# The attention's second products in three float32r passes for items 4 to 15

## The chip, the cores and the metric

One core of one Trainium2 chip runs the whole program. The time is the device time in microseconds of one execution; the time before is the median of three runs.

## The reference, cut to what matters

The kernel computes a linear attention, a mixture of eight experts with Sinkhorn-normalised gates, and a SwiGLU block, one behind the other, all in float32. The change touches the attention alone:

```python
def _attn_ref(q, k, v):            # 4 batches, 8 heads, 576 rows, 64 wide
    q_s = exp(q - max(q, axis=-1)); q_s = q_s / (sum(q_s, axis=-1) + 1e-9)
    k_s = exp(k - max(k, axis=2));  k_s = k_s / (sum(k_s, axis=2) + 1e-9)
    kv = einsum('bhsd,bhse->bhde', k_s, v)
    return einsum('bhsd,bhde->bhse', q_s, kv)
```

The last line is the product in question: each row of the softmaxed q times the 64x64 matrix kv of its head.

## The kernel before

The attention is cut into 16 items, each one batch and two heads. For an item, kv of the two heads is kept as one 128x128 block-diagonal tile (kvbd), and q is transposed to q^T, 128 partitions (two heads of 64) by two halves of 288 rows. The second product is then two float32 matmuls with kvbd as the weights and 288 moving columns each (x_mm, line 628), into two PSUM tiles px.

An item passes through small steps, each a function of its own: k_partial_max (m, line 471), q_max (qm, L480), q_sub (L489), k_max (a transpose on TensorE, L500), k_max2 (kmx, L507), k_spread (a matmul that needs kmx, L516), k_sub (ke, L523), the two exponentials (L511 and L532), k_sum, kv_mm (L566), k_total (L578), k_recip (kr, L586 and L587), kv_scale (kb, L596), q_norm (qs, L538 to L542), q_mul, q_T (transposes into two PSUM tiles pq, L606), q_T2 (c, L618), x_mm (X, L628), x_hi and x_lo (copies out of px, L643 to L650).

The order of the work on every engine is the order in which the program emits it (a manual schedule), and each engine's instructions run in that order. Items 0 to 3 are prepared by a list written out by hand (START). For items 4 to 15 a row of four strings (STEPS) is repeated, in which the number behind a step's name says how many items back it works:

```python
STEPS = (
    "D-1 ke-1 eq-1 ek-1 s-1", "G-2 K-2 kr-2 kb-2 m-0 T-2 qm-0 qp-0", "c-2 qs-1 qn-1",
    "B-0 kx-0 X-2 xh-2 xl-2",
)
```

These strings are laid between the units of the first expert layer: a unit h (two tiles ph_a of 12 float32r matmuls, relu on ScalarE into hh, L842, and on VectorE into hl, L843) and a unit y (four tiles py of 6 matmuls each; VectorE or ScalarE adds py into slot_e or a late tile, L905 and L903). One string goes ahead of each unit, one into the middle of a unit h, three behind the first three tiles of a unit y. Between them also stand the splits of weights into a high and a low part (split: a ScalarE copy to float32r, L94, and a VectorE subtract, L95; wsh_a, wsl_a, w2h, w2l) and the gates (L664 and L674, eight narrow matmuls each, copied out by L667 and L677).

The expert matmuls use mm3 (lines 97 to 100): for operands in two float32r parts it makes three passes, high by high, high by low, low by high. PSUM has two py tiles, two ph tiles, one pk and one pv tile, and two tiles of the pool psq, which pq and px share. Outside the START list px n takes the buffer in which pq n stood. qT has one buffer, kvbd two (even and odd items).

Of the kernel before, what the change touches and what calls it, by code (L numbers as in the profile page):

```python
# [8 lines left out]
F32 = mybir.dt.float32  # L9
F32R = mybir.dt.float32r  # L10
U32 = mybir.dt.uint32
AF = mybir.ActivationFunctionType
ALU = mybir.AluOpType
# [5 lines left out]
def kernel(  # L19
# [23 lines left out]
    nc = tc.nc  # L43
    nc = tc.nc
    B, H, S, D = q.shape
# [3 lines left out]
    P = 128  # L49
    SP = 96  # L50
    SC = S // SP
    H2 = S // 2
# [40 lines left out]
    def split(hi, lo, src, eng=None):  # L93
        nc.scalar.copy(hi, src)  # L94
        (eng or nc.vector).tensor_tensor(lo, src, hi.bitcast(F32), op=ALU.subtract)  # L95

    def mm3(ps, lh, ll, rh, rl, first, last):
        nc.tensor.matmul(ps, lh, rh, start=first, stop=False, skip_group_check=True)  # L98
        nc.tensor.matmul(ps, lh, rl, start=False, stop=False, skip_group_check=True)  # L99
        nc.tensor.matmul(ps, ll, rh, start=False, stop=last, skip_group_check=True)  # L100
# [13 lines left out]
    def bank(kind, cols, name):  # L114
        turn = BANK[kind]
        turn.append(turn.pop(0))
        pool = turn[-1]
        if isinstance(pool, str):
            return pb_tile(pool, name)[:, :cols]
        return pool.tile([P, cols], F32, tag="p", name=name)  # L120
# [317 lines left out]
    ap_ = attn.enter_context(tc.tile_pool(name="attn", bufs=2))  # L438
# [5 lines left out]
    }  # L444

    kvbd = []
    for i in range(2):
        t = ap_.tile([P, P], F32, tag=f"kvbd{i}", name=f"kvbd{i}", bufs=1)
        nc.gpsimd.memset(t, 0.0)
        kvbd.append(t)  # L450

    ITEMS = [(b, g) for b in range(B) for g in range(H // HG)]
# [137 lines left out]
    def kv_scale(i):  # L590
        st = ST[i]
        pkv, kr = st["pv"][:, :P], st["kr"]
        kv = kvbd[i % 2]
        for h in range(2):
            r = slice(h * D, (h + 1) * D)
            nc.scalar.activation(kv[r, r], pkv[r, r], AF.Copy, scale=kr[r])  # L596
        st["kv"] = kv

    def q_T(i):

# [12 lines left out]

    def q_T2(i):
        st = ST[i]
        qT = ap_.tile([P, 2, H2], F32, tag="qT", name=f"qT_{i}", bufs=1)
        for n, pq in enumerate(st["pq"]):
            nc.scalar.copy(qT[:, n], pq[:, :H2])  # L618
        st["qT"] = qT

    def x_mm(i, early=False):

        st = ST[i]
        st["px"] = []
        for n in range(2):
            nm = f"px_{i}_{n}"
            px = bank("y", 512, nm) if early else psq.tile([P, 512], F32, tag="pq", name=nm)
            nc.tensor.matmul(px[:, :H2], st["kv"], st["qT"][:, n], start=True, stop=True)  # L628
            st["px"].append(px)

    def x_parts(i, g0):
# [432 lines left out]
    def unit2_y(u, hook):  # L1064
# [22 lines left out]
    OPS = dict(  # L1087
        m=k_partial_max, B=k_max, kx=k_max2, D=k_spread, ke=k_sub, ek=k_exp, s=k_sum,
        G=kv_mm, K=k_total, kr=k_recip, kb=kv_scale, qm=q_max, qp=q_sub, eq=q_exp,
        qs=q_norm, qn=q_mul, T=q_T, c=q_T2, X=x_mm, xh=x_hi, xl=x_lo,  # L1090
    )

# [63 lines left out]
    for n, key in enumerate(keys):  # L1156
# [4 lines left out]
        i = 6 if kd == "a" else 13  # L1161
        if u >= NU and group(u)[0] == 0:
            i = 2 if kd == "a" else 5
# [105 lines left out]
    with tc.manual_schedule():  # L1269
# [59 lines left out]
        for step in START.split():  # L1329
            op, i = step.split("-")  # L1330
            if op in WOPS:
                WOPS[op](int(i))
            elif op == "X":
                x_mm(int(i), True)
            else:
                OPS[op](int(i))
# [23 lines left out]
        for i in range(13):  # L1360
            for j, st in enumerate(STEPS):
                if i == 0 and j == 0:
                    st = st.replace("D-1 ", "")
# [12 lines left out]
        n = 0  # L1376
# [82 lines left out]
```

## Time and profile before

| what | value |
|---|---|
| median of three runs | 2041.18 us (2040.77 to 2044.21) |
| the profiled execution | 2042.81 us |
| its span, first to last instruction | 2040.2 us |
| mean granted TensorE clock | 0.997 |
| TensorE matmul (PE) | 2011.4 us busy, 99% |
| TensorE weight load (PEld) | 1742.1 us, 85% |
| VectorE (DVE) | 1414.0 us, 69% |
| ScalarE (ACT) | 777.8 us, 38% |
| GpSimd (POOL) | 412.9 us, 20% |
| the chain that ended last | PE 94%, DVE 4%, ACT 1%, issue 1% |

Times in the trace are microseconds from the span's start. A matmul's record is longer than its turn on the engine: matmuls are pipelined, and the ends are modelled, so the distance between starts tells what one costs. An arrow in square brackets says how long an engine stood still before an instruction and what ended the wait.

### The profile page before, as it was taken

The page shows a single profiled execution, that of the slowest core. Times are in us where ns is not written, and L with a number is a line of the kernel's source. Part 1 is how long each engine was busy: PE and PEld are TensorE (multiplying, and loading weights), DVE is VectorE, ACT ScalarE, POOL GpSimd, SP SyncE. Part 2 cuts the span into 40 slices and gives each one's busy share as a digit, 9 for nine tenths or more (in the row PEclk, how much of TensorE's full clock was granted, in tenths as well). Part 3 has the DMA queues.
Part 4 walks back from the last instruction along what each step waited for, and adds up shares of the span by engine and source line. Part 5 has one row for each costly group of instructions (what it writes and reads, how often), then busy time and mean ns, then how long its engine had stood idle before and what let it go on. Part 6 is the DMA issues. An engine that isn't in the chain of part 4 may idle for free.

```text
span 2040.2 us, 25609 instructions
## 1 busy us (share of the span) xinstructions
PE 2011.4 (99%) x9522; PEld 1742.1 (85%) x9522; DVE 1414.0 (69%) x2178; ACT 777.8 (38%) x1374; POOL 412.9 (20%) x388
## 2 busy tenths in 40 slices
PE   7999999999999999999999999999999999999999
PEld 6888878888888888888888888888888888888887
DVE  8785787766767777776658878878764546565455
ACT  5454323335434334333343333333332243432432
POOL 5451000022222222222113223223220000110110
PEclk9999999999999999999999999999999999999999
DMA  8443222345666555565677778778874747656542
GB/s 206 128 126 104 83 93 93 99 147 196 224 241 220 197 205 205 210 222 206 224 286 263 263 261 289 275 273 292 283 263 156 273 153 259 226 201 260 199 159 77
DMA packets 154237, 415.09 MB, mean 203 GB/s; under 512 B 13569, under 2 KB 66305, under 8 KB 153729
## 3 DMA queue, kind: packets, MB, share of 16 engines
q1 hardware_dynamic: 154112, 413.47, 58.3%
q8 instruction: 74, 1.21, 0.2%
q14 instruction: 51, 0.41, 0.1%
HBM read 281.69 MB, written 131.73 MB: 203 GB/s over the span
## 4 chain that ended last, share of the span: by engine, by line
PE 94%; DVE 4%; ACT 1%; issue 1%; DMA 0%; POOL 0%; DVEq 0%; POOLq 0%; ACTq 0%
PE py L98 13%; PE py L99 12%; PE py L100 12%; PE b_a L100 10%; PE b_a L98 10%; PE b_a L99 10%; PE ph_a L98 3%; PE ph_a L100 3%; PE ph_a L99 3%; PE po L100 2%; PE po L99 2%; PE po L98 2%; PE b_v L98 2%; PE b_v L100 2%; PE b_v L99 2%; PE pv L566 1%
## 5 line engine op out<-in xcount | busy, mean ns | idle before, releaser
L98 PE MATMUL py<-w2h,hh 128*128 128x512 f32 x1152 | 453.7, 394 | 3.4 <-DVE slot_e L905 1.9
L99 PE MATMUL py<-w2l,hh 128*128 128x512 f32 x1152 | 450.0, 391 | 0.0
L100 PE MATMUL py<-w2h,hl 128*128 128x512 f32 x1152 | 449.5, 390 | 0.0
L781 ACT COPY u_a<-b_a 128x448 f32<-128x448 f32 x228 | 121.6, 533 | 693.9 <-PE b_a L100 693.8
L98 PEld LDWEIGHTS py<-w2h,hh 128*128 128x128 f32 x1152 | 216.7, 188 | 47.6 <-DVE slot_e L905 2.1
L100 PEld LDWEIGHTS py<-w2h,hl 128*128 128x128 f32 x1152 | 216.8, 188 | 45.9
L99 PEld LDWEIGHTS py<-w2l,hh 128*128 128x128 f32 x1152 | 216.9, 188 | 42.8
L98 PE MATMUL b_a<-sT,wsh_a 128*128 128x448 f32 x608 | 220.1, 362 | 3.3 <-DVE c L795 2.1
L100 PE MATMUL b_a<-sT,wsl_a 128*128 128x448 f32 x608 | 220.7, 363 | 0.0
L99 PE MATMUL b_a<-sT,wsh_a 128*128 128x448 f32 x608 | 220.3, 362 | 0.0
L909 DVE SCALAR_TENSOR_TENSOR slot_a<-py,Pm,slot_a 128x512 f32<-128x512 f32 x217 | 162.5, 749 | 52.2 <-PE py L100 50.2
L909 DVE SCALAR_TENSOR_TENSOR slot_b<-py,Pm,slot_b 128x512 f32<-128x512 f32 x217 | 161.2, 745 | 23.5 <-PE py L100 22.5
L100 PE MATMUL b_a<-sB,wsl_a 128*128 128x448 f32 x456 | 165.7, 363 | 0.2 <-DMA wsl_a<-wdl_a 0.2
L99 PE MATMUL b_a<-sB,wsh_a 128*128 128x448 f32 x456 | 165.2, 362 | 0.0
L98 PE MATMUL b_a<-sB,wsh_a 128*128 128x448 f32 x456 | 165.2, 362 | 0.0
L95 DVE TENSOR_TENSOR w2l<-w2r,w2h 128x512 fp32r<-128x512 f32 x162 | 117.9, 728 | 41.3 <-ACT w2h L94 41.3
L843 DVE SCALAR_TENSOR_TENSOR hl<-c,hh 128x896 fp32r<-128x896 f32 x128 | 143.2, 1119 | 0.9 <-ACT hh L842 0.7
L805 POOL TENSOR_TENSOR c<-u_a,p_a 128x448 f32<-128x448 f32 x64 | 73.9, 1155 | 344.4 <-ACT u_a L781 344.3
L240 POOL TENSOR_TENSOR sum<-w1r 128x256 f32<-128x256 f32 x32 | 23.8, 744 | 570.8 <-DMA w1r<-in_moe_w_dram 261.8
L842 ACT ACTIVATE hh<-c 128x896 fp32r<-128x896 f32 x128 | 122.4, 956 | 28.0 <-POOL c L805 28.0
L94 ACT CAST w2h<-w2r 128x512 fp32r<-128x512 f32 x162 | 97.1, 618 | 92.1 <-PE py L100 83.2
L98 PEld LDWEIGHTS b_a<-sT,wsh_a 128*128 128x128 f32 x608 | 113.8, 187 | 13.2 <-DVE c L795 3.7
(232 smaller groups left out, 3680.5 us busy)
## 6 DMA issues: line engine op xcount, KB each, us to landing
w2r<-in_moe_w_dram SPq DMA_DIRECT2D x96, 512.0 KB, 4.5
w1r<-in_moe_w_dram SPq DMA_DIRECT2D x64, 512.0 KB, 3.4
wsdh<-wsh_a SPq DMA_DIRECT2D x32, 896.0 KB, 6.5
wsdl<-wsl_a SPq DMA_DIRECT2D x32, 896.0 KB, 7.9
wsh_a<-wsdh SPq DMA_DIRECT2D x32, 896.0 KB, 6.5
wsl_a<-wsdl SPq DMA_DIRECT2D x32, 896.0 KB, 8.5
w2d<-w2l SPq DMA_DIRECT2D x32, 512.0 KB, 2.9
w2l<-w2d SPq DMA_DIRECT2D x32, 512.0 KB, 5.1
```

The lines of the kernel that those rows point to most:

```text
L94: nc.scalar.copy(hi, src)
L95: (eng or nc.vector).tensor_tensor(lo, src, hi.bitcast(F32), op=ALU.subtract)
L98: nc.tensor.matmul(ps, lh, rh, start=first, stop=False, skip_group_check=True)
L99: nc.tensor.matmul(ps, lh, rl, start=False, stop=False, skip_group_check=True)
L100: nc.tensor.matmul(ps, ll, rh, start=False, stop=last, skip_group_check=True)
L240: nc.gpsimd.tensor_tensor(s1, a21, a22, op=ALU.add)
L566: nc.tensor.matmul(st["pv"][:, :P], st["ke"][:, c].rearrange("p h d -> p (h d)"), st["v"][:, :, c, :], start=(c == 0), stop=(c == SC - 1),)
L781: nc.scalar.copy(tmp[n], bk[i])
L805: nc.gpsimd.tensor_tensor(c[:, 1, 1], tmp["u3"], tmp["p5"], op=ALU.add)
L842: nc.scalar.activation(th, src, AF.Relu)
L843: return lambda: nc.vector.scalar_tensor_tensor(tl, src, 0.0, th.bitcast(F32), op0=ALU.max, op1=ALU.subtract)
L909: nc.vector.scalar_tensor_tensor(a, py, pe, a, op0=ALU.mult, op1=ALU.add)
```

## The change

For items 4 to 15 kv and q^T are each kept in two float32r parts, and x_mm makes three passes of mm3 for each half in place of one float32 matmul. kv_scale writes the high part on ScalarE and then, for each half of the diagonal, the low part on VectorE, in one scalar_tensor_tensor that scales again and subtracts. q_T2 calls split for each half. The two new kv tiles, kh and kl, have one buffer each; ql has one. Items 0 to 3 work as before, with q^T in the tile that is now declared float32r and used as float32.

```diff
     kvbd = []
-    for i in range(2):
-        t = ap_.tile([P, P], F32, tag=f"kvbd{i}", name=f"kvbd{i}", bufs=1)
-        nc.gpsimd.memset(t, 0.0)
+    for i in range(4):
+        t = ap_.tile([P, P], F32 if i < 2 else F32R, tag=f"kvbd{i}", name=f"kvbd{i}", bufs=1)
+        nc.gpsimd.memset(t if i < 2 else t.bitcast(F32), 0.0)
         kvbd.append(t)
...
     def kv_scale(i):
...
+        kh, kl = kvbd[2:]
         for h in range(2):
             r = slice(h * D, (h + 1) * D)
-            nc.scalar.activation(kv[r, r], pkv[r, r], AF.Copy, scale=kr[r])
-        st["kv"] = kv
+            nc.scalar.activation(kh[r, r], pkv[r, r], AF.Copy, scale=kr[r])
+            nc.vector.scalar_tensor_tensor(
+                kl[r, r], pkv[r, r], kr[r], kh[r, r].bitcast(F32), op0=ALU.mult, op1=ALU.subtract
+            )
+        st["kv"] = kh, kl
...
     def q_T2(i):
...
+        qT = ap_.tile([P, 2, H2], F32R, tag="qT", name=f"qT_{i}", bufs=1)
+        ql = ap_.tile([P, 2, H2], F32R, tag="ql", name=f"ql_{i}", bufs=1)
         for n, pq in enumerate(st["pq"]):
-            nc.scalar.copy(qT[:, n], pq[:, :H2])
-        st["qT"] = qT
+            split(qT[:, n], ql[:, n], pq[:, :H2])
+        st["qT"] = qT, ql
...
     def x_mm(i, early=False):
...
-            nc.tensor.matmul(px[:, :H2], st["kv"], st["qT"][:, n], start=True, stop=True)
+            if i < 4:
+                nc.tensor.matmul(px[:, :H2], st["kv"], st["qT"][:, n], start=True, stop=True)
+            else:
+                (kh, kl), (qh, ql) = st["kv"], st["qT"]
+                mm3(px[:, :H2], kh, kl, qh[:, n], ql[:, n], True, True)
```

## Rows read from the trace of the kernel before

**Rows 1.** Windows, 49 to 189 us: length, busy of PE, PEld, DVE, ACT, POOL, clock, DMA.

```profile
49.00:189.00 140.00, 136.60 (x761) 115.75 (x759) 103.13 (x178) 70.91 (x156) 60.84 (x54) 0.98 0.37 113
```

**Rows 2.** Waits, 50 to 190 us: total, times, longest.

```profile
PE py L98 <- DVE slot_e L905: 1.9, 2, 1.3
PE py L98 <- DVE late L905: 1.2, 1, 1.2
...
DVE hl L843 <- ACT hh L842: 12.8, 8, 2.6
```

**Rows 3.** Timeline of TensorE: start us, us, engine line op; item 14, and ph_a.

```profile
175.29 1.13 PE L628 MATMUL px<-qT,kvbd 128*128 128x288 f32 x4
176.26 0.28 PE L674 MATMUL pg<-wg,slot_b 128*128 128x8 f32 x2
...
61.29 0.40 PE L98 MATMUL ph_a<-slot_a,wsh_a 128*128 128x512 f32 x1
61.52 0.39 PE L99 MATMUL ph_a<-slot_a,wsh_a 128*128 128x512 f32 x1
```

**Rows 4.** Instructions of lines 650 and 843: duration ns min/median/max, starts, shape.

```profile
L650 DVE TENSOR_TENSOR slot_a<-px,slot_a x8: 359/412/425, 23.8 to 35.1; 128x256 fp32r<-128x256 f32 x8
...
L843 DVE SCALAR_TENSOR_TENSOR hl<-ph_a,hh x64: 676/691/693, 39.1 to 445.9; 128x512 fp32r<-128x512 f32 x64
```

**Rows 5.** Timeline of item 9, 111.5 to 115 us: VectorE, ScalarE, TensorE's px.

```profile
111.55 0.16 DVE L587 RECIPROCAL kr<-kr 128x1 f32<-128x1 f32 x1
111.63 1.53 DVE L471 TENSOR_REDUCE m<-k 96x128 f32<-96x768 f32 x1
...
111.80 0.63 ACT L596 ACTIVATE kvbd<-pv,kr 64x64 f32<-64x64 f32 x2 [2.16 <-DVE kr L587]
...
112.46 0.70 ACT L618 COPY qT<-pq 128x288 f32<-128x288 f32 x2
...
113.08 0.93 DVE L480 TENSOR_REDUCE qm<-q 96x12 f32<-96x768 f32 x1
...
113.56 1.16 PE L628 MATMUL px<-qT,kvbd 128*128 128x288 f32 x4
...
113.94 0.67 DVE L905 TENSOR_TENSOR slot_e<-py,slot_e 128x512 f32<-128x512 f32 x1
...
114.54 0.93 DVE L538 TENSOR_REDUCE qs<-qe 96x12 f32<-96x768 f32 x1
```

**Rows 6.** Timelines of VectorE and TensorE, item 4: kmx and its reader.

```profile
54.32 0.25 DVE L507 TENSOR_REDUCE kmx<-pk 128x1 f32<-128x96 f32 x1
...
54.62 0.46 PE L516 MATMUL pk<-ident,kmx 128*96 128x128 f32 x2
```

**Rows 7.** Timelines of VectorE and TensorE, item 5.

```profile
64.23 0.69 DVE L843 SCALAR_TENSOR_TENSOR hl<-ph_a,hh 128x512 fp32r<-128x512 f32 x1 [1.62 <-ACT hh L842]
...
69.00 0.50 PE L98 MATMUL py<-w2h,hh 128*128 128x512 f32 x1 [0.64 <-DVE slot_e L905]
```

**Rows 8.** Timelines of VectorE and TensorE, item 6.

```profile
75.44 0.67 DVE L905 TENSOR_TENSOR slot_e<-py,slot_e 128x512 f32<-128x512 f32 x1
...
76.71 1.16 PE L628 MATMUL px<-qT,kvbd 128*128 128x288 f32 x4
```

**Rows 9.** Timelines of VectorE and TensorE, items 7 and 13: evictions and py.

```profile
88.55 0.69 PE L98 MATMUL py<-w2h,hh 128*128 128x512 f32 x1 [1.26 <-DVE slot_e L905]
...
163.05 0.68 DVE L905 TENSOR_TENSOR late<-py,late 128x512 f32<-128x512 f32 x1
...
163.78 0.50 PE L98 MATMUL py<-w2h,hh 128*128 128x512 f32 x1
```

**Rows 10.** Windows, a stretch at half clock (columns as in rows 1).

```profile
88.70:92.10 3.40, 3.40 (x9) 2.56 (x10) 2.35 (x7) 0.00 (x0) 2.40 (x2) 0.50 0.37 105
```

**Rows 11.** Timeline of GpSimd at the start.

```profile
1.35 0.20 POOL L449 MEMSET kvbd<- 128x128 f32 x1
...
6.38 1.47 POOL L489 TENSOR_TENSOR qe<-q,qm 96x768 f32<-96x768 f32 x1 [4.83 <-DVE qm L480]
```

More of the change, by code (lines that the diff above doesn't have):

```diff
@@ L592, in kv_scale @@
         pkv, kr = st["pv"][:, :P], st["kr"]
-        kv = kvbd[i % 2]
+        if i < 4:
+            kv = kvbd[i % 2]
+            for h in range(2):
+                r = slice(h * D, (h + 1) * D)
+                nc.scalar.activation(kv[r, r], pkv[r, r], AF.Copy, scale=kr[r])
+            st["kv"] = kv
+            return
+        kh, kl = kvbd[2:]
         for h in range(2):
             r = slice(h * D, (h + 1) * D)
-            nc.scalar.activation(kv[r, r], pkv[r, r], AF.Copy, scale=kr[r])
-        st["kv"] = kv
+            nc.scalar.activation(kh[r, r], pkv[r, r], AF.Copy, scale=kr[r])
[3 more added lines that the diff above has]
+        st["kv"] = kh, kl
     def q_T(i):
@@ L615, in q_T2 @@
         st = ST[i]
-        qT = ap_.tile([P, 2, H2], F32, tag="qT", name=f"qT_{i}", bufs=1)
+        if i < 4:
+            qT = ap_.tile([P, 2, H2], F32R, tag="qT", name=f"qT_{i}", bufs=1).bitcast(F32)
+            for n, pq in enumerate(st["pq"]):
+                nc.scalar.copy(qT[:, n], pq[:, :H2])
+            st["qT"] = qT
+            return
+        qT = ap_.tile([P, 2, H2], F32R, tag="qT", name=f"qT_{i}", bufs=1)
+        ql = ap_.tile([P, 2, H2], F32R, tag="ql", name=f"ql_{i}", bufs=1)
         for n, pq in enumerate(st["pq"]):
-            nc.scalar.copy(qT[:, n], pq[:, :H2])
-        st["qT"] = qT
+            split(qT[:, n], ql[:, n], pq[:, :H2])
+        st["qT"] = qT, ql
     def x_mm(i, early=False):
@@ L627, in x_mm @@
             px = bank("y", 512, nm) if early else psq.tile([P, 512], F32, tag="pq", name=nm)
-            nc.tensor.matmul(px[:, :H2], st["kv"], st["qT"][:, n], start=True, stop=True)
+            if i < 4:
+                nc.tensor.matmul(px[:, :H2], st["kv"], st["qT"][:, n], start=True, stop=True)
+            else:
+                (kh, kl), (qh, ql) = st["kv"], st["qT"]
+                mm3(px[:, :H2], kh, kl, qh[:, n], ql[:, n], True, True)
             st["px"].append(px)
```

## The prediction

> **What bounds the kernel now.** I read the attention stretch first, because the change touches nothing else: 49 to 189 us holds the work of items 4 to 15. TensorE is busy 136.60 of those 140 us and VectorE 103.13 [rows 1]. By busy time TensorE is the bound and VectorE has room; the next views say why that is not the whole story. The list of waits shows three waits of TensorE, all for evictions of py, 3.1 us together, while VectorE's own largest is 12.8 us, for ScalarE's relu in front of hl [rows 2]. So VectorE idles mostly at one kind of place, and a delay on its queue costs nothing only if that place comes before TensorE next needs it. The timelines around single items answer that, item by item.
>
> **The products themselves.** An item's two f32 products stand as four records of 288 columns; they begin at 175.29 and the next matmul's at 176.26, so 0.97 us [rows 3]. The new item has six float32r passes of 288 columns. A float32r pass of 512 columns follows the last after 0.23 us [rows 3]. The columns alone at 2.4 GHz are 0.213 and 0.120 us; with the same 0.013 to 0.017 us on top, 288 columns come to 0.133 us. Bounds: 0.129 (0.23 by the share of columns) and 0.23 (no gain for fewer columns); I take 0.133, as the columns set the 0.23. Six are 0.80 us: 0.17 us less per item, 2.0 us for twelve items, if nothing waits.
> The Trainium skill ("TensorE: Matmul & The Clock Gate", section "Back-to-back issue gap") gives N/2.4 + 2.5 ns when warm, so 122.5 ns for 288 columns and an estimated 0.235 us an item, 2.8 us in all. It gives 216 ns for 512 columns where the row has 230, so I keep the row.
>
> **The added VectorE work.** kv_scale now emits, per half, a ScalarE write of kh and a VectorE scalar_tensor_tensor of kl, 64x64 from PSUM. Nearest rows: a reciprocal of one column 0.16 us, a reduce over 96 columns 0.25 us; I take 0.20. q_T2 adds two subtracts of 128x288 from PSUM. The same operation on 256 columns takes 0.41 us, a scalar_tensor_tensor of 512 takes 0.69 [rows 4]: 0.45 by the line between, bounds 0.41 and 0.69. Back to back a VectorE instruction starts some 0.08 us before its predecessor ends (row 113.08, 0.93 long, against 113.94) [rows 5], so each subtract costs 0.37 us of queue.
>
> **What that does to the queue.** Item 9 [rows 5]. The reciprocal of kr ends at 111.71 and today m starts at 111.63. ScalarE's two kvbd writes run from 111.80 to 112.43. New: kl of the first half can start only after 112.11, that of the second after 112.43, so it ends near 112.43 + 0.04 + 0.20 = 112.67, and m, next in VectorE's order, starts near 112.60. **The step kb costs VectorE 0.97 us**, more than half of it standing still for ScalarE, with everything behind it (m, qm, evictions, hl). **The step c costs 2 x 0.37 = 0.74 us** more, emitted ahead of qs.
> X needs both: today it needs qT, which ScalarE had at 113.16. New, m, qm and the eviction at 113.94 end 0.97 us later, at 115.58, and the two subtracts end at 115.95 and 116.32. The px tiles take the two PSUM banks in which pq stood (two buffers), and the subtract now reads pq, so the three passes of px 0 start after the first subtract and those of px 1 after the second. The last three end at 116.37 + 2 x 0.133 + 0.30 = 116.94, where 0.30 is the 0.39 of a 512-column record less 224 columns at 2.4 GHz. Today px ends at 114.72. TensorE is in order, so all of its work moves by **+2.2 us**.
>
> The other items, each taken from a point where both engines are equally late (VectorE waits for TensorE or ScalarE again before the next kr):
> - Items 4 and 10: kmx ends at 54.57 and the k_spread matmul that needs it starts at 54.62 [rows 6]. kmx is behind both steps, so TensorE stands 0.97 + 0.74 = 1.71 us longer. Two items: +3.4.
> - Items 5, 8, 11, 14: VectorE waits 1.62 us in front of hl [rows 7], which swallows the 0.97 (14 has no m behind it). The subtracts then go in after hl, and the eviction for which TensorE already waits 0.64 us at 69.00 comes 0.74 us later. Four items: +3.0. 8 and 11 have kmx close before the spread instead, for the same price.
> - Item 6: the eviction of 75.44 moves to 76.41, the second subtract ends near 77.82 and px near 78.43 where it ended at 77.87 [rows 8]: +0.6.
> - Item 7: TensorE waits 1.26 us for the eviction at 88.55 [rows 9], which is behind kb but ahead of c: 0.97 - 0.17 = +0.8.
> - Item 13: the eviction that ends at 163.73 is followed by the py matmul at 163.78 [rows 9] and stands behind both steps: +1.7.
> - Items 12 and 15: qT is made long before X, so the faster passes show: -0.3 together.
> Sum: 2.2 + 3.4 + 3.0 + 0.6 + 0.8 + 1.7 - 0.3 = **+11.4 us**.
>
> **The clock.** In this part TensorE ran twice for some 3.4 us at 1.2 GHz; in the first of them it was busy all of the 3.40 us at a granted clock of 0.50 [rows 10], so it cost half of that, 1.7 us. Each time it fell while TensorE was waiting for an eviction, behind narrow gate matmuls; after the shorter wait of item 5 it did not fall. The change adds waits as long as these (item 9's, item 4's), so I count two more: +3.4 us; bounds none and four.
>
> **Costed at nothing.** Two more memsets on GpSimd, 0.20 us each: its next work waits 4.83 us for qm at 6.38 [rows 11]. Without that cover they would cost 0.4 us. The q^T of the first four items changes only its declared type. kh and kl are one pair where there were two kvbd tiles, but kb of an item is emitted after X of the item before, and waits for a later matmul of TensorE anyway. After 189 us no operation changes, and TensorE stays the engine in front, so the loss should stay. No DMA is added or moved; loads issued behind k_sub and kv_mm move with those.
>
> **Sum.** 11.4 + 3.4 = 14.8 us. The profiled execution took 2042.81 us (span 2040.2), 1.63 above the median of the three runs; against the median 2041.18 that is 2056 us.
>
> **Rivals.**
> A, hidden: VectorE has 37 us without work in the stretch, about 3 an item, against 1.7 added. If its idle time falls between each delay and TensorE's next need, only the passes show: 2041.2 - 2.0 = 2039.2. For it: items 5 and 8, where the wait before hl takes up the first delay. Against it: kmx, 0.05 us ahead of its reader, and item 9, where VectorE runs without a gap from kr to qs. It decides at the subtracts of c: if ql is there when X begins, A holds.
> B, half: the delays overlap more than I add (a late TensorE lets VectorE catch up, subtracts at their lower bound) and no clock is lost: half of 11.4, 2047.
> C, faster: A holds, and moving the evictions also removes both half-clock stretches: 2039.2 - 2 x 1.7 = 2035.8. For it: these depend on where waits fall. Against it: both sit behind evictions that now come later.
> D, the passes aren't cheaper: at 0.23 us each, six cost 1.38 against 0.97. Where X waits, three passes after the last subtract cost 0.3 more; elsewhere it is 0.6 an item: about 5 us on top, 2061.
>
> **How the numbers follow.** 0.2% is 4.1 us, about what a measurement of this kernel can tell from no change. Chances: my forecast 0.64, B 0.10, D 0.06 (all slower: 0.80), A 0.15 (within), C 0.05 (faster). The range runs from 2044, between A and B, to 2064: above, the clock's bound adds 3.4 and the subtracts' bound (0.69 for 0.45, felt by some nine items twice) up to 4.3, the lesser pass prices the rest. Left out are A and C, 0.20.
>
> **What would show it.** In the changed profile: px as six records an item, near 0.13 us apart where nothing waits; kl starting some 0.4 us after the reciprocal, and m 0.97 us later against it; TensorE waits named after ql in front of px, about 2 us for item 9; kmx in front of L516 and L905 in front of py with larger totals than the 3.1 us; further stretches at 1.2 GHz. I'd be wrong if px followed its predecessor without a gap in items 4, 9 and 10, or if m kept its place right behind the reciprocal.

## The result and the profile after

The changed kernel is slower: 2063.41 us (median of four runs, 2060.81 to 2065.0) against 2041.72 us (the kernel before, with a fourth run), a ratio of 1.0102 with a 95% interval of 1.009 to 1.0114. The sign and the range of the prediction held, and the mechanism in the main; the size, +14.8 us forecast against +21.7 us measured, was too small by a third.

The page of the changed kernel, first lines:

```profile
span 2061.3 us, 25707 instructions
## 1 busy us (share of the span) xinstructions
PE 2015.6 (98%) x9546; PEld 1744.9 (85%) x9546; DVE 1430.8 (69%) x2226; ACT 778.0 (38%) x1374; POOL 411.6 (20%) x390
```

The span grew by 21.1 us. VectorE got 16.8 us of work more. TensorE was busy 4.2 us longer, so 16.9 of the 21.1 us are time in which it stood still. Where it arose is seen by taking TensorE's instructions without px, which are the same in both kernels, and comparing the start of each with its twin:

```
ahead of item 4    +0.9 us     after item 11    +15.8
after item 6       +6.4        after item 12    +15.4
after item 9      +12.4        after item 15    +19.9, and so up to 290 us
                               end of the span  +21.1
```

The 0.9 us ahead of item 4 arises in the first 26 us; the profiles of the twelve experiments stand between -0.03 (e4, the whole change) and +0.7 there, with the same list of steps, so I don't count it to the change. Of the last 1.2 us, 1.0 arises where Sinkhorn's serial part runs, around 315 us, with 6.8 us at half clock there in place of 3.4. The other 19.0 us are items 4 to 15, as forecast.

The list of waits of the changed kernel, TensorE's, 49 to 210 us (total, times, longest; line numbers are those of the changed kernel):

```profile
PE px L98 <- DVE ql L95: 10.4, 9, 1.6
PE py L98 <- DVE slot_e L926: 3.5, 2, 2.8
PE py L98 <- DVE late L926: 2.6, 3, 1.3
PE pk L500 <- DVE m L471: 1.7, 3, 1.3
PE py L98 <- DVE lg L698: 1.6, 1, 1.6
```

Where three waits of 3.1 us stood [rows 2], there are 18 of 19.8 us, and all five lines name VectorE. VectorE's own list for the same stretch:

```profile
DVE kvbd L604 <- ACT kvbd L603: 10.0, 24, 0.5
...
DVE hl L864 <- ACT hh L863: 6.2, 5, 1.8
```

The 12.8 us of idle time in front of hl [rows 2] are half gone; 10.0 us of a new kind have come, in kb, where kl waits for kh. Item 9, which answers to [rows 5], VectorE first and then TensorE:

```profile
121.02 0.16 DVE L587 RECIPROCAL kr<-kr 128x1 f32<-128x1 f32 x1
121.64 0.28 DVE L604 SCALAR_TENSOR_TENSOR kvbd<-pv,kr,kvbd 64x64 fp32r<-64x64 f32 x1 [0.46 <-ACT kvbd L603]
122.29 0.29 DVE L604 SCALAR_TENSOR_TENSOR kvbd<-pv,kr,kvbd 64x64 fp32r<-64x64 f32 x1 [0.38 <-ACT kvbd L603]
122.61 1.48 DVE L471 TENSOR_REDUCE m<-k 96x128 f32<-96x768 f32 x1
124.00 0.95 DVE L480 TENSOR_REDUCE qm<-q 96x12 f32<-96x768 f32 x1
124.98 0.69 DVE L926 TENSOR_TENSOR slot_e<-py,slot_e 128x512 f32<-128x512 f32 x1
125.59 0.81 DVE L95 TENSOR_TENSOR ql<-pq,qT 128x288 fp32r<-128x288 f32 x2
```

```profile
124.24 0.27 PE L500 MATMUL pk<-ident,m 96*128 96x96 f32 x1 [1.30 <-DVE m L471]
126.09 0.40 PE L98 MATMUL px<-qT,kvbd 128*128 128x288 f32 x1 [1.58 <-DVE ql L95]
126.33 0.29 PE L99 MATMUL px<-ql,kvbd 128*128 128x288 f32 x1
126.46 0.29 PE L100 MATMUL px<-qT,kvbd 128*128 128x288 f32 x1
...
126.86 0.29 PE L100 MATMUL px<-qT,kvbd 128*128 128x288 f32 x1
126.99 0.39 PE L98 MATMUL ph_a<-slot_a,wsh_a 128*128 128x512 f32 x1
```

m starts 1.43 us after the reciprocal's end (121.18), where it started 0.08 us before it. TensorE stands still twice, first for m and then for ql. From the second of the six passes on they are 0.13 us apart, as forecast.

Item 4's kb, ScalarE, shows why kl is so late:

```profile
50.19 0.31 ACT L603 ACTIVATE kvbd<-pv,kr 64x64 fp32r<-64x64 f32 x1
50.84 0.31 ACT L603 ACTIVATE kvbd<-pv,kr 64x64 fp32r<-64x64 f32 x1 [0.34 <-DVE kvbd L604]
```

The second write of kh waits for VectorE's first kl, so the two engines take turns: 0.31, 0.28, 0.31, 0.29 us one behind the other.

### The profile page after: what moved, and what is told of

Its sections match the earlier page's. It is cut to its first block, busy times and chain, and to the rows that moved or that the text cites. A ratio compares the mean times of both kernels' runs of the same rounds, so it can differ in the third digit from the quotient of the medians.

```text
span 2061.3 us, 25707 instructions
## 1 busy us (share of the span) xinstructions
PE 2015.6 (98%) x9546; PEld 1744.9 (85%) x9546; DVE 1430.8 (69%) x2226; ACT 778.0 (38%) x1374; POOL 411.6 (20%) x390
## 4 chain that ended last, share of the span: by engine, by line
PE 91%; DVE 6%; ACT 1%; issue 1%; DMA 1%; POOL 0%; ACTq 0%; DVEq 0%; POOLq 0%
PE py L98 12%; PE py L99 12%; PE py L100 12%; PE b_a L100 10%; PE b_a L99 10%; PE b_a L98 10%; PE ph_a L98 3%; PE ph_a L100 3%; PE ph_a L99 3%; PE po L100 2%; PE po L98 2%; PE po L99 2%; PE b_v L98 2%; PE b_v L100 2%; PE b_v L99 2%
```

## The experiments

Each batch (e1 to e4, e5 to e8, e9 and e10, e11 and e12) ran beside the kernel before on one chip; the medians of before were 2041.5 us for e1 to e4, 2042.8 for e5 to e8 and 2042.4 for e9 to e12. Theory Q: the time is lost because VectorE's queue is longer. W: px's wait for ql is the loss.

**e1, the passes alone.**

```diff
-            nc.vector.scalar_tensor_tensor(kl[r, r], ...)
...
-        ql = ap_.tile([P, 2, H2], F32R, tag="ql", name=f"ql_{i}", bufs=1)
-            split(qT[:, n], ql[:, n], pq[:, :H2])
+            nc.scalar.copy(qT[:, n], pq[:, :H2])
...
-                mm3(px[:, :H2], kh, kl, qh[:, n], ql[:, n], True, True)
+                mm3(px[:, :H2], kh, kh, qh[:, n], qh[:, n], True, True)
```

> The changed kernel without any of the added VectorE work: kl and ql are not made, and all six passes of an item are kh by q^T's high part (the low parts of the product are left out). Theory Q (the loss is VectorE's queue): only the cheaper passes are left, 6 x 0.133 against 0.97 us, so 2.0 us less than before over twelve items, about 2040 us, within 3 us of before either way because of stretches at half clock; the shift of TensorE against before grows in no item. Rival P (the passes, the new tiles or the place of the tiles cost the time): near the changed kernel, 2055 us or more.

Measured: 2041.05 us, ratio 0.9996 (0.9986 to 1.0005). The passes and tiles cost nothing, P falls. But they don't give 2.0 us either: by its profile TensorE gains 0.6 us over items 4 to 15, because it arrives earlier at VectorE's results and waits there: its waits from 49 to 210 us make 4.3 us, where they made 3.1. So even low parts that cost nothing would not make this change worth a measurable amount.

**e2 and e3, one part each.** e2 has kl and no ql, e3 has ql and no kl:

```diff
 e2
-            split(qT[:, n], ql[:, n], pq[:, :H2])
+            nc.scalar.copy(qT[:, n], pq[:, :H2])
-                mm3(px[:, :H2], kh, kl, qh[:, n], ql[:, n], True, True)
+                mm3(px[:, :H2], kh, kl, qh[:, n], qh[:, n], True, True)
 e3
-            nc.vector.scalar_tensor_tensor(kl[r, r], ...)
-                mm3(px[:, :H2], kh, kl, qh[:, n], ql[:, n], True, True)
+                mm3(px[:, :H2], kh, kh, qh[:, n], ql[:, n], True, True)
```

> The changed kernel with kl but without ql: the pass with q^T's low part multiplies its high part again (that part of the product is left out). The trace of the changed kernel has kr's reciprocal ending at 50.09 and m starting at 51.50, 1.49 us later against it than before, not the 0.97 of the forecast, because kvbd's second half on ScalarE starts only after VectorE's first kl. Theory Q: that delay reaches TensorE in items 4, 7, 9, 10 and 13 (1.2 to 1.5 us each) and is swallowed in front of hl in 5, 8, 11 and 14: about +6 us, 2045 to 2051. Rival W (the loss is the wait of px for ql alone): within 3 us of before.

> The changed kernel with ql but without kl: the pass with kl multiplies kh again (that part of the product is left out). Theory Q: the two subtracts add 0.74 us to VectorE's queue and px waits for them where they end late: 0.7 us each in items 4, 5, 8, 10, 11, 13 and 14, 1.2 in item 9, little in the others: about +6 us, 2045 to 2051. With e2 that is less than the changed kernel's +22, as the two delays add up only where both are felt. Rival W (px's wait for ql is the whole loss): near the changed kernel, 2058 or more.

Measured: e2 2050.88 us, ratio 1.0042 (1.0028 to 1.0056); e3 2047.11 us, ratio 1.003 (1.0019 to 1.0041). W falls: without any ql, kl alone costs 9 us. TensorE's waits in e2, 49 to 210 us, stand at kmx, evictions and m:

```profile
PE pk L516 <- DVE kmx L507: 4.4, 5, 1.3
PE py L98 <- DVE slot_e L925: 3.5, 2, 2.8
PE pk L500 <- DVE m L471: 1.7, 3, 1.3
...
```

9.4 and 5.6 us make 15.0, less than the 21.7 of both together. I read this so: each delay alone is partly taken up by VectorE's idle time, the second is not.

**e4, both writes of kh ahead of both kl.**

```diff
         for h in range(2):
             r = slice(h * D, (h + 1) * D)
             nc.scalar.activation(kh[r, r], pkv[r, r], AF.Copy, scale=kr[r])
+        for h in range(2):
+            r = slice(h * D, (h + 1) * D)
             nc.vector.scalar_tensor_tensor(
```

> The whole change, but kb emits both ScalarE writes of kh first and then both VectorE instructions for kl. Theory Q with the back-and-forth of the engines as the mis-sized term: ScalarE's two writes stand back to back again, kl's second ends some 1.1 to 1.3 us after the reciprocal in place of 1.4, and about ten items gain 0.15 to 0.3 us each: 2 to 4 us less than the changed kernel, 2059 to 2061. Rival: the order is of no account, since VectorE has to wait for ScalarE anyway: within 1 us of the changed kernel.

Measured: 2062.23 us, ratio 1.0098 (1.0083 to 1.0113): the rival, my expectation missed. VectorE in item 4, whose reciprocal ends at 49.12, and ScalarE's writes:

```profile
48.96 0.16 DVE L587 RECIPROCAL kr<-kr 128x1 f32<-128x1 f32 x1
49.90 0.58 DVE L606 SCALAR_TENSOR_TENSOR kvbd<-pv,kr,kvbd 64x64 fp32r<-64x64 f32 x2 [0.77 <-ACT kvbd L603]
50.51 1.55 DVE L471 TENSOR_REDUCE m<-k 96x128 f32<-96x768 f32 x1
...
49.22 0.64 ACT L603 ACTIVATE kvbd<-pv,kr 64x64 fp32r<-64x64 f32 x2
```

ScalarE's writes stand back to back, yet the first kl waits for both, and m starts 1.39 us after the reciprocal. In either order the four instructions run one at a time, and their sum is nearly the same (m 1.39 us behind the reciprocal for 1.41).

**e5, kl without kh.**

```diff
-                kl[r, r], pkv[r, r], kr[r], kh[r, r].bitcast(F32), op0=ALU.mult, op1=ALU.subtract
+                kl[r, r], pkv[r, r], kr[r], kvbd[0][r, r], op0=ALU.mult, op1=ALU.subtract
```

> The changed kernel, but kl is taken against the unused float32 tile kvbd 0 in place of kh, so it reads nothing that ScalarE writes (kl is then not the low part of kv; the amount of work is the same). Both instructions still read the PSUM tile pv. Theory V (readers of one PSUM tile on two engines are put in order of emission): ScalarE and VectorE still take turns, and m starts some 1.4 us after the reciprocal ends; time as the changed kernel within 2 us, 2061 to 2065. Theory T (kl waits for kh alone, as its data demand): kl starts within 0.1 us of the reciprocal, m some 0.5 to 0.6 us after it; about 0.85 us less in the queue for each of ten items, 5 to 9 us less than the changed kernel, 2054 to 2058.

Measured: 2062.6 us, ratio 1.0101 (1.0084 to 1.0117): theory V. VectorE in item 4:

```profile
49.12 0.16 DVE L587 RECIPROCAL kr<-kr 128x1 f32<-128x1 f32 x1
49.72 0.28 DVE L604 SCALAR_TENSOR_TENSOR kvbd<-pv,kr,kvbd 64x64 fp32r<-64x64 f32 x1 [0.44 <-ACT kvbd L603]
50.37 0.29 DVE L604 SCALAR_TENSOR_TENSOR kvbd<-pv,kr,kvbd 64x64 fp32r<-64x64 f32 x1 [0.38 <-ACT kvbd L603]
```

Each kl still waits for ScalarE, though it reads nothing that ScalarE writes in this item. What the two still have in common is what both read, pv in PSUM and kr; the program puts these reads on two engines in the order of emission. I take pv to be the reason; pv and kr weren't told apart. The Trainium skill ("PSUM — Partial Sum Buffer", Terms) forbids two engines in the same bank and quadrant at once, reads included, and allows different quadrants. The two halves lie in partitions 0 to 63 and 64 to 127, so by that page the wait of kh's second half for kl's first is more than is needed. No run here shows that rule: a kernel without this wait wasn't tried.

**e6, X one string later.**

```diff
-        "D-1 ke-1 eq-1 ek-1 s-1", "G-2 K-2 kr-2 kb-2 m-0 T-2 qm-0 qp-0", "c-2 qs-1 qn-1",
-        "B-0 kx-0 X-2 xh-2 xl-2",
+        "X-3 xh-3 xl-3 D-1 ke-1 eq-1 ek-1 s-1", "G-2 K-2 kr-2 kb-2 m-0 T-2 qm-0 qp-0", "c-2 qs-1 qn-1",
+        "B-0 kx-0",
...
-        for i in range(13):
-            for j, st in enumerate(STEPS):
+        for i in range(14):
+            for j, st in enumerate(STEPS if i < 13 else STEPS[:1]):
```

> The whole change, but X and the copies out of px are emitted one string later (ahead of the next item's k_spread), so that ql has one unit more of TensorE's work to be ready in. Theory Q (a longer VectorE queue that TensorE meets at several places): px's waits for ql, 10.4 us in the changed kernel, nearly vanish, but kmx, m and the evictions stay late, and part of the wait shows there: 2049 to 2056. Rival Y (VectorE's queue as a whole is the bound of the stretch, and the place where TensorE waits is of no account): within 4 us of the changed kernel, 2059 or more. Rival W (px's wait is the loss): 2045 or less.

Measured: 2062.89 us, ratio 1.0102 (1.0087 to 1.0117). Rival Y, and my expectation of 2049 to 2056 missed: not a microsecond came back. TensorE's waits, 49 to 212 us:

```profile
PE pk L516 <- DVE kmx L507: 7.0, 6, 1.4
PE py L98 <- DVE late L926: 3.7, 2, 1.9
PE py L98 <- DVE slot_e L926: 3.5, 2, 2.8
...
PE px L98 <- DVE ql L95: 0.3, 2, 0.2
```

px's 10.4 us became 0.3, and kmx took 7.0. A wait at px is only the first place at which TensorE notices that VectorE is late.

**e7, kl on GpSimd.**

```diff
-            nc.scalar.activation(kh[r, r], pkv[r, r], AF.Copy, scale=kr[r])
-            nc.vector.scalar_tensor_tensor(kl[r, r], ...)
+            nc.scalar.activation(kvbd[i % 2][r, r], pkv[r, r], AF.Copy, scale=kr[r])
+            nc.scalar.copy(kh[r, r], kvbd[i % 2][r, r])
+            nc.gpsimd.tensor_tensor(kl[r, r], kvbd[i % 2][r, r], kh[r, r].bitcast(F32), op=ALU.subtract)
```

> The whole change, with kl made off VectorE: ScalarE writes kv in float32 as before and copies it to kh, GpSimd subtracts kh from it. VectorE has nothing to do in kb. Theory Q: what is left is ql's part, as in e3: 2045 to 2050, and m stands right behind the reciprocal again. Rival G (GpSimd, with 61 of 140 us busy, gives kl so late that px waits for it, or delays q_sub and q_mul): 2055 or more.

Measured: 2048.69 us, ratio 1.003 (1.0018 to 1.0042). That is e3's cost, with the whole product computed: with kb off VectorE, 5.9 us are left of the change's 21.7.

**e8, the kernel before with idle work on VectorE.**

```diff
+    fill = ap_.tile([P, 640], F32, tag="fill", name="fill", bufs=1)
+    nc.gpsimd.memset(fill, 0.0)
...
         st["kv"] = kv
+        if i >= 4:
+            for _ in range(2):
+                nc.vector.tensor_tensor(fill, fill, fill, op=ALU.subtract)
```

> The kernel before, with two idle VectorE instructions of 128x640 elements behind each kb of items 4 to 15 that nobody reads and that wait for nothing: about 0.73 us each in the queue, 1.47 together, as long as the changed kernel's kb takes from VectorE. The f32 products are as before. Theory Q (the time on VectorE's queue counts, whatever fills it): as e2 with the dearer products, 2050 to 2054. Rival S (the loss comes from the two engines' taking turns or from the wait of px, not from time on the queue): within 4 us of before.

Measured: 2057.69 us, ratio 1.0076 (1.0061 to 1.0091). Q, though larger than expected, and S falls: two instructions an item that wait for nothing and that nobody reads cost 15 us. The fill itself was larger than I had planned, 1.67 us in item 9 and 2.57 in item 4 in place of 1.47:

```profile
49.49 2.57 DVE L603 TENSOR_TENSOR fill<-fill 128x640 f32<-128x640 f32 x2
...
118.53 1.67 DVE L603 TENSOR_TENSOR fill<-fill 128x640 f32<-128x640 f32 x2
```

**e9 and e10, w2's low parts on GpSimd**, in e7 and in the kernel before:

```diff
-            split(W2[u][0][:, f], W2[u][1][:, f], rv[:, f])
+            split(W2[u][0][:, f], W2[u][1][:, f], rv[:, f], nc.gpsimd if u < 9 else None)
```

> e7 (the whole change, kl off VectorE), and the low parts of w2 of units 1 to 8, 16 subtracts of 128x512 at 0.68 us, made on GpSimd instead of VectorE. Theory Q: about 10 us of VectorE's queue are taken out of a stretch in which the change put 9 us (ql) in, so most of e7's loss comes back: 2040 to 2045. Rival G: GpSimd takes 1.2 us or more for each, the two engines slow each other down as they did beside e8's fill (1.57 us beside a GpSimd addition against 0.81 alone), or w2's low part comes too late for py: 2048 or more.

> The kernel before with the same 16 subtracts on GpSimd. Theory Q: if VectorE's queue is what TensorE meets in this stretch even before the change, the 3.1 us of waits for evictions shrink and one or both stretches at half clock go (1.2 to 1.7 us each): 2036 to 2041. Rival G as for e9, or VectorE's queue cost nothing more before: 2041 to 2045.

Measured: e9 2048.72 us, ratio 1.0029 (1.0018 to 1.004); e10 2042.92 us, ratio 1.0003 (0.9994 to 1.0012). Q as I had put it fails in both: VectorE was relieved of 16 instructions, and nothing came back. e9's time lies where rival G had put it, and a subtract took 1.26 to 1.30 us on GpSimd, as G had said; but all waits of TensorE in e9 name VectorE, with e7's sums (3.7, 1.9, 1.3 and 1.3 us), so no wait shows GpSimd late. The wait in front of hl from 49 to 210 us, first e7's and then e9's:

```profile
DVE hl L865 <- ACT hh L864: 15.1, 11, 2.7
```

```profile
DVE hl L865 <- ACT hh L864: 30.0, 14, 3.3
```

The w2 subtracts stand ahead of hl, where VectorE would have waited anyway. The theory had to be narrowed to R: what counts is the run of VectorE from kr up to the next thing that TensorE needs.

**e11 and e12, w1's low parts on GpSimd instead**, again in e7 and in the kernel before. In items 4, 7, 10 and 13 they stand inside that run, ahead of ql; in the others ahead of an eviction.

```diff
-            task("y", u - 2, part, lambda u=u, part=part: w1_split(u, part))
+            task("y", u - 2, part, lambda u=u, part=part: w1_split(u, part, nc.gpsimd if u < 9 else None))
```

> e7 (the whole change, kl off VectorE) with the low parts of w1 of units 2 to 8, 14 subtracts of 128x512, on GpSimd, where e9 had moved those of w2. Theory R (what counts is VectorE's run from kr to the next instruction for which TensorE waits; work that stands ahead of the wait for hl is free, as in e9): the w1 subtracts stand inside that run, ahead of ql in items 4, 7, 10 and 13 and ahead of an eviction in the others, so unlike w2's they give time back: the 3.2 us of waits for evictions go, and 0.5 us each in two or three px waits: 2043 to 2046. Rival L (no work taken off VectorE gives anything back, since the waits are set by other engines): within 1.5 us of e7's 2048.7. Rival G (GpSimd delivers w1's low part too late for ph_a): 2050 or more, with TensorE waits named after wsl_a.

> The kernel before with the same 14 subtracts on GpSimd. Theory R: the 3.1 us of waits for evictions shrink by two thirds or more, and one or both stretches at half clock with them (1.2 to 1.7 us each): 2036 to 2040, less than before's 2042.4. Rival L: within 1.5 us of before. Rival G: 2044 or more.

Measured: e11 2041.69 us, ratio 0.9995 (0.9986 to 1.0004), 7 us less than e7 and more than R had said; e12 2038.93 us, ratio 0.9983 (0.9974 to 0.9992). L and G fall. Fourteen subtracts of the same shape as e9's sixteen gave back all of e7's loss, for standing elsewhere: in e7 these fourteen had taken 13.0 us on VectorE and e9's sixteen 13.8, and on GpSimd both took some 1.3 us each. Of the 7 us, 5.2 arise in the attention by the profiles, where e7 also has a stretch at half clock (at 146 us, worth at most 1.7) that e11 has not. TensorE's waits in e11 and in e12, 49 to 210 us:

```profile
PE px L98 <- DVE ql L95: 2.3, 6, 0.5
PE py L98 <- DVE late L927: 0.7, 2, 0.4
PE ph_a L100 <- POOL wsl_a L95: 0.7, 2, 0.4
PE py L98 <- DVE slot_e L927: 0.6, 1, 0.6
```

```profile
PE pk L516 <- DVE kmx L507: 1.5, 1, 1.5
PE py L98 <- DVE slot_e L905: 0.6, 1, 0.6
PE ph_a L100 <- POOL wsl_a L95: 0.4, 1, 0.4
```

Neither has a stretch at half clock in the attention any more. e12 is faster than both kernels; it is the kernel before with that one edit, without the change, and 3.5 us below it.

## Why the prediction was right or wrong

- **The bound.** Right: the room that VectorE's 103 us of 140 seemed to leave was not where the change needed it. e1 (no loss without VectorE's work) and e8 (the loss without the passes) show it from both sides.
- **The passes.** The price was right (0.133 us between records), the gain was not: 2.0 us forecast, 0.6 us in e1. The 122.5 ns of the Trainium skill ("TensorE: Matmul & The Clock Gate", section "Back-to-back issue gap") stays below the row again. A faster engine only gained as far as the next result of the slower one.
- **kb.** This step was too small, by an overlap that doesn't happen: "kb costs VectorE 0.97 us" measured 1.49. I let kh's second write run beside the first kl (0.72 us from the reciprocal to the end of both writes, plus one kl of 0.20). The four instructions come one at a time in either order (e4) and without kh's data too (e5; I take their common reads of pv to be the reason), so they add up, and kl took 0.28 and 0.29 us for my 0.20, above the 0.25 of the nearest row. In items 4, 6, 7, 9, 10 and 13 it adds 0.52 each: 3.1 us.
- **Items 5, 8, 11 and 14.** I gave item 5's 1.62 us in front of hl to all four. It holds for item 5, where the shift grew by 0.7 as forecast. In item 8 VectorE waited 0.51 us there before the change and the shift grew by 1.6 us, in item 11 it waited 0.69 us and the shift grew by 1.4: 1.5 us more than forecast in the two. That was to be read from the same timeline, one item further on.
- **c and px's banks.** Right: ql takes 0.45 us each, and px's first pass starts behind the first subtract. Items 9 and 10 grew by 3.0 and 2.0 us for 2.2 and 1.7. The places were mostly wrong: I had px late in items 6 and 9 and TensorE waiting at kmx in 4 and 10 and at evictions in 5, 8, 11 and 14; in the changed kernel nine items wait in front of px, 10.4 us, and no wait at kmx is in the list.
- **Sum.** Forecast 11.4; with the two corrections (3.1 and 1.5) about 16.0. Measured 19.0 in the stretch, in which one stretch at half clock more stood (three, at 56, 97 and 196 us, for two), 1.7 us at most by the price of [rows 10]. Of the rest, over 1 us, item 12 makes some 0.9: I had it among the two items that gain 0.3 us together, since "qT is made long before X", but X now needs ql, TensorE waited 0.76 us for it and the shift grew by 0.8. What is left stays open. The range reached up to 2064, 0.6 us above the measured time; its upper part was meant for a greater loss of clock and for dearer subtracts, and neither came, so that the range held is in part luck.
- **The clock.** Two more were forecast: one came inside the attention, at most 1.7 us, and 3.4 us more at half clock at 315 us, where 1.0 us arose: together at most 2.7 of the 3.4 us. I had counted one for each new wait as long as those behind which it fell in the kernel before (items 9 and 4), and that doesn't hold: in item 4 the granted clock fell to 0.50 (1.2 GHz) at 56.03 behind a wait of 1.58 us for ql, in item 9 it did not fall behind waits of 1.30 and 1.58, and at 195.98 it fell behind a wait of 0.32. Nor does the sum of the waits set their number: the kernel before has two in the attention with 3.1 us of waits, e3 has one with 8.2, e11 none with 4.3. The cause stays open.
- **Rivals.** A and C needed ql to be there when X begins, and it was 1.6 us late in item 9; e6 shows that even then A would not have come true, since I had it decide at the wrong place: without px's wait, kmx and the evictions waited. B falls by the time, D by the records.

The rows for items 4, 12 and 14 of the changed kernel, and the wait in front of hl in item 8 of the kernel before:

```profile
55.06 0.40 PE L98 MATMUL px<-qT,kvbd 128*128 128x288 f32 x1 [1.58 <-DVE ql L95]
165.00 0.40 PE L98 MATMUL px<-qT,kvbd 128*128 128x288 f32 x1 [0.76 <-DVE ql L95]
195.86 0.71 PE L98 MATMUL py<-w2h,hh 128*128 128x512 f32 x1 [0.32 <-DVE late L926]
```

```profile
102.69 0.69 DVE L843 SCALAR_TENSOR_TENSOR hl<-ph_a,hh 128x512 fp32r<-128x512 f32 x1 [0.51 <-ACT hh L842]
```

## What to carry to other kernels

Before work goes onto an engine that is "69% busy", follow its queue from the place of the new work to the next result that the bounding engine waits for: idle time ahead of that result hides it, idle time behind it doesn't, and busy shares don't tell the two apart (the same subtract was worth nothing in one place and half a microsecond in another). In e6 a stall that was removed by moving its reader came back at the next readers; taking work out of the run (e7, e11, e12) removed it. Check each occurrence of a repeating pattern, as its slack may differ by a factor of three.

## What the runs showed that I had not expected

VectorE's fill of 128x640, two inputs in SBUF, took 0.81 us alone (item 5 of e8) and 1.57 us where a GpSimd addition had started just before it (item 4):

```profile
62.39 0.81 DVE L603 TENSOR_TENSOR fill<-fill 128x640 f32<-128x640 f32 x1
...
49.37 1.01 POOL L558 TENSOR_TENSOR s<-ke 96x384 f32<-96x384 f32 x1 [3.11 <-ACT ke L535]
49.49 1.57 DVE L603 TENSOR_TENSOR fill<-fill 128x640 f32<-128x640 f32 x1
```

The Trainium skill ("SBUF — State Buffer", section "Who interferes with whom") says that a VectorE instruction with two SBUF inputs contends with a GpSimd instruction that reads SBUF, and that the later one blocks. The rows agree: the fill's extra 0.76 us is about what was left of the addition that began at 49.37 and took 1.01. The kernel before has the same in w1's subtracts, which take 0.68 us (at 53.72) and 1.40 us where a GpSimd instruction is already running:

```profile
66.32 1.47 POOL L547 TENSOR_TENSOR qe<-qe,qs 96x768 f32<-96x768 f32 x1 [2.37 <-DVE qs L542]
66.94 1.40 DVE L95 TENSOR_TENSOR wsl_a<-w1r,wsh_a 128x512 fp32r<-128x512 f32 x1
```

Work that is moved to GpSimd can so slow down what stays on VectorE; in e11 and e12 the move paid all the same.
